# W = w3 @ w_out in float32 matmuls, with its two weights narrowed straight into place

## The chip, the core and the metric

The kernel runs on one core of one Trainium2 chip. The metric is the device time of one execution in microseconds, as a median of repeated runs. The engines are TensorE (PE in the profile, its weight loads PEld), VectorE (DVE), ScalarE (ACT), GpSimd (POOL) and SyncE (SP), which issues the DMAs.

## What is computed

The reference runs three layers, one behind the other, over 3072 tokens of width 384 (4 sequences of 768, 8 heads of 48):

```
# 1. linear attention with decay w and bonus u, per head a 48x48 state
y[t] = r[t] @ (state + (u*k[t]) v[t]);  state = w*state + k[t] v[t]
# 2. mixture of 8 experts: one expert per token, tokens with x @ w_skip <= 0 pass through
out = x + gate * (relu(x @ w1[e]) @ w2[e])
# 3. second MLP, d_ff = 1024
h = (x @ w1) * (x @ w2) @ w3
return (h @ w_out).astype(np.float32)
```

In layer 3 nothing stands between `@ w3` and `@ w_out`, so the kernel computes the 1024x384 product W = w3 @ w_out once and uses `(a*b) @ W`. Its weights w1, w2, w3 and w_out arrive as float64 and are narrowed to float32 on the chip.

## The kernel before

The program has three stages, each in an order of instructions that is written out by hand; every engine takes its own in that order.

**Attention** goes over 24 tiles of 128 tokens (two chunks of 64, of two sequences). The loop at L822 runs n = 0 to 21; the last two tiles and the last routing are done step by step in the list at L875, called the tail here. Iteration n prepares tile n+2 (`prep` L392: DVE writes FB, POOL writes kt; `prep_k` L406: POOL writes ku), computes the scores of tile n+1 on PE (`scores` L450) and masks them on DVE (`evac` L459), then computes y of tile n (`y_mm` L465), transposes tile n-1 and takes its router logits (PE output T), and updates the state (`ds_mm` L480, PE output S). The routing of a group of tiles (`route_a`, `route_b`, `route_c`) adds some twenty small DVE instructions to five of the iterations.

**W** is made in between. A job is a quarter of w_out (L310, "o") or a row block of w3 ("3"); there are 4 and 8. `w_step` (L703), called two or three times in an iteration, takes a job on by one step: ACT makes the magnitude (`magnitude` L117), DVE does three instructions on a work tile `nar` (`narrow` L126: L133, L136, L140), then ACT casts the high part (L167, `wo_hi` or `w3_hi`) and POOL subtracts for the low part (L171, `wo_lo` or `w3_lo`), while DVE is at the next job. All 12 low parts go to POOL, by `w_eng` (L700) and LOP. `w_mm` (L728) gives the matmuls of W one by one: a row block takes 24 of 384 columns, three for each of the 8 contraction blocks (high by high, high by low, low by high), in float32r, which is one pass each. The finished block is split again into W_hi (ACT, L713) and W_lo (DVE, L721).

**Filling.** PE is not kept busy by the attention's small matmuls. `fill_at` (L760) stands behind each pair of them and keeps an account, `debt`, of how many columns are wanted (a rate R[n] for each iteration, in columns per microsecond) and how many were issued. Where the account is positive it puts in a burst: three matmuls of W, or, as long as W's weights are not ready, six matmuls of 256 columns on zeros (`idle_mm`, L753; called dummies here). `keep` (L771) puts in a fixed number of them in the tail.

**Experts** start at L915 with the gather of the first tokens (`load_x`, DMA `xr`), their transposes (`pT`) and a loop over 64 pieces of weights (`mm1` PE output hp, `mm2` PE output y). What is left of W is done between those transposes and the first `mm1` (L948). **The second MLP** (L1162) follows.

Of the kernel before, what the change touches and what calls it, by code (L numbers as in the profile page):

```python
# [18 lines left out]
P = 128  # L19
# [21 lines left out]
R = (1180, 1060, 950, 1000, 1030, 1150, 1150, 1090, 1150, 1000, 1150, 1180, 1300, 1240, 1270, 1350, 1350, 1210, 1400, 1400, 1400, 1270, 1270)  # L41
# [10 lines left out]
KW = 4  # L52
W0 = 3
# [22 lines left out]
def fused_kernel(ctx, tc, att, rk, vn, wt, u, wg, we, w3, wo, w12, r, k, v, wu, out):  # L76
# [14 lines left out]
    # an expert's slots: gate, the token to read, the token to write (none: out of bounds)  # L91
# [14 lines left out]
    def load_wide(pool, tag, src):  # L106
        """Loads [P, n] of a weight and gives it as float32."""
        k = src.shape[1]
        if not wide:
            raw = pool.tile([P, k], F32, tag=tag, name=tag, bufs=2)  # L110
            nc.sync.dma_start(out=raw, in_=src)
            return raw
        raw = pool.tile([P, k, 2], I32, tag=tag, name=tag, bufs=2)
        nc.sync.dma_start(out=raw.rearrange("p n w -> p (n w)"), in_=src.bitcast(I32))
        return raw

    def magnitude(raw, pool):  # L117
        """First step of narrowing float64 words, (low, high) pairs. The high word as a float32 has the upper 8 of the
        float64's 11 exponent bits: 2^-112 less is 1023 - 127 less in all 11."""
        if not wide:  # L120
            return raw
        t = pool.tile([P, raw.shape[1]], I32, tag="nar", name="nar", bufs=2)
        nc.scalar.activation(out=t.bitcast(F32), in_=raw[:, :, 1].bitcast(F32), func=AF.Abs, scale=2.0 ** -112)
        return t

    def narrow(raw, t):  # L126
        """The other steps, and where the result is."""
        if not wide:
            return [], t
# [13 lines left out]
        return [shift, low, sign], t.bitcast(F32)  # L143

    def prep_steps(jobs, pool, eng):
        """Weights made ready as high and low parts, in steps of about one instruction on VectorE, the other engines'
        for the weights before and after between them. A job: what was loaded, a function that gives the places of high
        and low or None if it can't yet, what to do when the load was read, when high is there and when low is."""
        back = []

        def front():
            job = next(jobs, None)
            return job and job + (magnitude(job[0], pool),)
# [26 lines left out]
        while job:  # L180
            raw, places, used, end_hi, end_lo, t = job
            ops, x = narrow(raw, t)
# [35 lines left out]
    def ring_pair():  # L218
        # the last pieces leave ring 0 to the way into the second MLP
# [8 lines left out]
    # ------------------------------------------------------------ attention  # L228
# [3 lines left out]
    wo_hi = wop.tile([P, NF, D], F32R, name="wo_hi")  # L232
    wo_lo = wop.tile([P, NF, D], F32R, name="wo_lo")
# [8 lines left out]
    with tc.manual_schedule():  # L242
# [7 lines left out]
        # natural-layout decay of even chunks, the bonus u, the decay of odd chunks  # L250
# [67 lines left out]
        # decay tables: U[:, h, i] = w^(i-64), Tm[:, h, j] = w^(63-j)  # L318
# [35 lines left out]
        # of each token: its number + 1 in two parts, its gate in three  # L354
        val = ac.tile([P, NT, 5], BF16, name="val")

        def consts():
            """Constants that the first tiles don't need; in steps."""
# [25 lines left out]
        # ---- per chunk pieces  # L384
# [7 lines left out]
        def prep(n):  # L392
            """Decayed r and k: r into both planes of F."""
# [12 lines left out]
        def prep_k(n):  # L406
            c2 = n // 2 % 2
            kn = blobs[n][:, D:2 * D]
            # the last chunks' states are of no use
# [55 lines left out]
        def y_mm(n, tag="y"):  # L465
# [6 lines left out]
            for h in range(NH):  # L472
                # the next head's first columns ride along
# [85 lines left out]
        def route_b(gi):  # L559
            """A token's rank in its expert: the tokens before, in the tile and in the tiles before."""  # L560
# [23 lines left out]
        def route_c(gi):  # L584
            """Of a token's slot: the lane, and whether it is in one of the 16 tiles (beyond CAP: no such lane)."""
# [15 lines left out]
        def route_d(gi, eng):  # L601
            """The gate's parts."""
# [23 lines left out]
        def place(k, t):  # L626
            """What the slots of the next tokens get."""
# [19 lines left out]
        def place_all(gi, eng):  # L647
            """The last ones: first the tokens' numbers."""
# [31 lines left out]
        # ---- W = w3 @ w_out: weights made ready in small steps, matmuls between the attention's  # L680
        w3_ = {}

        def w_jobs():
            """w_out's quarters and w3's row blocks."""
            for i, (kind, q) in enumerate(jobs):
                def places(kind=kind, q=q):
                    if kind == "o":
                        return [a[:, 2 * q:2 * q + 2].rearrange("p g d -> p (g d)") for a in (wo_hi, wo_lo)]
                    if q - 2 >= n_w[0]:
                        return None  # L690
                    w_eng[0] = nc.gpsimd if q < 4 or LOP[q - 4] else nc.vector
                    w3_[q] = [wop.tile([P, NF, P], F32R, tag=x, name=x, bufs=2) for x in ("w3_hi", "w3_lo")]
                    return [a.rearrange("p g f -> p (g f)") for a in w3_[q]]

                yield (raw_w.pop(0), places, lambda i=i: load_w(i + 2), lambda j=(kind + "h", q): fresh[1].append(j),
                       lambda j=(kind, q): fresh[1].append(j))
# [3 lines left out]
        w_eng = [nc.gpsimd]  # L700
        wprep = prep_steps(w_jobs(), nrp, lambda: w_eng[0])
# [7 lines left out]
        def w_evac(k):  # L709
            """Takes a finished row block of W out of PSUM."""  # L710
# [17 lines left out]
        def w_mm():  # L728
            for f in range(NF):
                ps = None  # L730
                i = 0
                for g, low in [(g, False) for g in range(NF)] + [(g, True) for g in range(NF)]:
                    while not (("3", f) in done if low else ("o", g // 2) in done and ("3h", f) in done):
                        yield False
                    if ps is None:
# [5 lines left out]
                        hi, lo = w3_.pop(f)  # L741
                    for a, b in ((lo, wo_hi),) if low else ((hi, wo_hi), (hi, wo_lo)):
                        nc.tensor.matmul(ps, a[:, g], b[:, g], start=(i == 0), stop=(i == 3 * NF - 1))  # L743
                        i += 1
                        yield True
# [4 lines left out]
        debt = [0.0, 0]  # L750
# [9 lines left out]
        def fill_at(us, act):  # L760
            """Part of W, or of nothing while W's weights are not ready, where the matmuls in between (their time, and
            columns with rows and passes as weights) are too thin for the tensor engine's clock to stay up."""
            debt[0] += rate[0] * us - act
            if debt[0] >= 0:
                for _ in range(BURST):
                    debt[1] = bool(next(wmm, None))
                    if not debt[1]:
                        idle_mm()
                debt[0] += BURST * (rate[0] * (0.163 if debt[1] else 0.218) - (384 if debt[1] else 512))

        def keep(k):  # L771
            """Matmuls of W, or of nothing."""
            for _ in range(k):
                if not next(wmm, None):
                    idle_mm()

        # ---- pipeline
# [92 lines left out]
        # the last two, with the banks that are free now  # L870
# [29 lines left out]
        # general path wanted: a decay out of the tables' range, or an expert with over CAP tokens  # L900
# [5 lines left out]
    # ------------------------------------------------------------ experts  # L906
# [510 lines left out]
```

## Time and profile before

| | |
|---|---|
| median of 3 runs | 709.45 us (708.15 to 711.8) |
| span of the profiled execution | 712.7 us |
| PE busy in the span | 648.3 us (91%) |
| DVE busy | 431.4 us (61%) |
| ACT busy | 290.5 us (41%) |
| POOL busy | 234.3 us (33%) |

The profile gives the span of one execution, from its first instruction to its last, and nothing of what lies around it; that span is 3.25 us above the median of the three timed runs. The shares are means over stages that differ. The attention's loop lasts until about 207 us, its tail until 238 us, the experts until 401 us, and the second MLP to the end. A row of the timeline gives the start and the duration of an instruction. A small float32 matmul leaves two records, one behind the other.

### The profile page before, as it was taken

How to read it: one execution, taken by the hardware profiler on the slowest of the kernel's cores; microseconds unless marked ns; L12 is line 12 of the kernel's file. 1: busy time of each engine (PE TensorE's matmuls, PEld its weight loads, DVE VectorE, ACT ScalarE, POOL GpSimd, SP SyncE). 2: the span in 40 equal slices, each digit the busy share in tenths (PEclk: the TensorE clock that was granted, in tenths of full speed). 3: DMA queues.
4: the chain of work that ended last, by engine and by line, in shares of the span. 5: the costliest groups of instructions: out<-in, count | busy, mean ns of one | idle time of the engine just before them, and what ended most of it. 6: DMA issues, size and time to landing. Idle time of an engine off the chain costs nothing.

```text
span 712.7 us, 13497 instructions
## 1 busy us (share of the span) xinstructions
PE 648.3 (91%) x5398; PEld 577.3 (81%) x5398; DVE 431.4 (61%) x705; ACT 290.5 (41%) x634; POOL 234.3 (33%) x175
## 2 busy tenths in 40 slices
PE   8798588697898899989988999999999999999996
PEld 6677476586687799989988789889889889889886
DVE  8779999998998668989987432132232231230330
ACT  4556554544463465656643422232232222221220
POOL 7889658634643355556632200000000000000000
PEclk9888768878999899999999999999999999999999
DMA  8998778677531687776851100200200100101001
GB/s 203 274 244 245 193 208 228 196 203 204 161 112 28 228 287 228 245 264 236 273 194 61 62 1 17 72 1 22 67 1 34 56 1 34 55 1 46 0 1 49
DMA packets 32647, 89.71 MB, mean 126 GB/s; under 512 B 5257, under 2 KB 19226, under 8 KB 31552
## 3 DMA queue, kind: packets, MB, share of 16 engines
q1 hardware_dynamic: 30528, 83.33, 38.6%
q0 software_dynamic: 2048, 5.44, 2.2%
q8 instruction: 44, 0.72, 0.4%
q14 instruction: 27, 0.22, 0.1%
HBM read 77.02 MB, written 12.58 MB: 126 GB/s over the span
## 4 chain that ended last, share of the span: by engine, by line
PE 54%; DVE 22%; DMA 10%; issue 9%; POOL 2%; ACT 2%; SPq 0%; DVEq 0%; POOLq 0%; ACTq 0%
PE ab L1182 28%; PE po L1200 14%; DMA TB<-in_att 5%; PE hp L983 3%; DVE nar L136 3%; DVE elo L102 2%; PE wp L743 2%; PE y L1002 2%; DMA raw<-in_we 2%; DVE nar L140 2%; DVE nar L133 2%; DVE hl L987 1%; DVE FB L463 1%; DVE FB L403 1%; DVE FB L462 1%
## 5 line engine op out<-in xcount | busy, mean ns | idle before, releaser
L1182 PE MATMUL ab<-bxh,w12h 128*128 128x512 f32 x288 | 112.4, 390 | 0.6 <-ACT bxh L1220 0.6
L1182 PE MATMUL ab<-bxh,w12l 128*128 128x512 f32 x288 | 112.1, 389 | 0.0
L1182 PE MATMUL ab<-bxl,w12h 128*128 128x512 f32 x288 | 112.0, 390 | 0.0
L1189 DVE TENSOR_TENSOR p_sb<-ab,a_sb 128x512 f32<-128x512 f32 x48 | 33.2, 692 | 123.5 <-PE ab L1182 123.5
L1190 ACT CAST ph<-p_sb 128x512 fp32r<-128x512 f32 x48 | 29.8, 620 | 105.7 <-DVE p_sb L1189 105.7
L1200 PE MATMUL po<-W_hi,ph 128*128 128x384 f32 x192 | 66.7, 348 | 0.0
L1200 PE MATMUL po<-W_hi,pl 128*128 128x384 f32 x192 | 65.0, 339 | 0.0
L1200 PE MATMUL po<-W_lo,ph 128*128 128x384 f32 x192 | 65.0, 338 | 0.0
L983 PE MATMUL hp<-xh,ehi 128*128 128x256 f32 x192 | 56.5, 296 | 8.9 <-DVE hl L987 8.8
L1182 PEld LDWEIGHTS ab<-bxh,w12h 128*128 128x128 f32 x288 | 54.1, 188 | 12.6 <-ACT bxh L1220 1.6
L1182 PEld LDWEIGHTS ab<-bxl,w12h 128*128 128x128 f32 x288 | 54.1, 188 | 11.7 <-DVE bxl L1222 0.4
L1182 PEld LDWEIGHTS ab<-bxh,w12l 128*128 128x128 f32 x288 | 54.1, 188 | 10.8
L411 POOL TENSOR_TENSOR ku<-blob,KU 128x768 f32<-128x768 f32 (+1 forms) x24 | 47.6, 1985 | 36.5 <-PE S L489 27.7
L983 PE MATMUL hp<-xl,ehi 128*128 128x256 f32 x192 | 54.7, 287 | 0.0
L983 PE MATMUL hp<-xh,elo 128*128 128x256 f32 x192 | 54.6, 287 | 0.0
L101 ACT CAST ehi<-raw 128x768 fp32r<-128x768 f32 x64 | 52.6, 828 | 4.5 <-DMA raw<-in_we 4.5
L1191 DVE TENSOR_TENSOR pl<-p_sb,ph 128x512 fp32r<-128x512 f32 x48 | 33.2, 693 | 32.9 <-ACT ph L1190 32.9
L102 POOL TENSOR_TENSOR elo<-raw,ehi 128x768 fp32r<-128x768 f32 x22 | 42.4, 1927 | 20.1 <-ACT ehi L101 19.8
L986 ACT ACTIVATE hh<-hp 128x256 fp32r<-128x256 f32 x64 | 24.6, 385 | 56.9 <-PE hp L983 56.7
L439 ACT ACTIVATE zv<-VS,z 128x48 f32<-128x48 f32 x184 | 43.9, 321 | 8.4 <-DVE z L426 6.3
L475 PE MATMUL y<-VS,FB 112*64 112x64 f32 (+3 forms) x384 | 32.0, 240 | 16.3 <-ACT VS L447 10.7
L983 PEld LDWEIGHTS hp<-xh,ehi 128*128 128x128 f32 x192 | 37.6, 197 | 11.4 <-DVE hl L987 11.3
(221 smaller groups left out, 1667.4 us busy)
## 6 DMA issues: line engine op xcount, KB each, us to landing
raw<-in_we SPq DMA_DIRECT2D x32, 768.0 KB, 5.0
TB<-in_att SPq DMA_DIRECT2D x48, 192.0 KB, 5.6
blob<-in_rk SPq DMA_DIRECT2D x24, 384.0 KB, 6.5
raww<-in_w SPq DMA_DIRECT2D x8, 1024.0 KB, 6.6
raw<-in_w SPq DMA_DIRECT2D x8, 768.0 KB, 6.7
VS<-in_vn SPq DMA_DIRECT2D x24, 192.0 KB, 3.6
xm<-xg SPq DMA_DIRECT2D x48, 96.0 KB, 3.3
out<-ob SPq DMA_DIRECT2D x24, 192.0 KB, 1.9
```

Of the source, the lines that this page charges most:

```text
L101: nc.scalar.copy(out=hi, in_=raw)
L102: (eng or nc.vector).tensor_tensor(out=lo, in0=raw, in1=hi.bitcast(F32), op=ALU.subtract)
L411: nc.gpsimd.tensor_tensor(out=ku_[n][:, a:b], in0=kn[:, None, :].to_broadcast([P, b - a, D]), in1=KU[:, c2 + a:c2 + b], op=ALU.mult)
L439: nc.scalar.activation(out=zv[:, h], in_=vs[:, 0, h], func=AF.Copy, scale=z[:, h:h + 1])
L475: nc.tensor.matmul(yv[0:64, h, 0:w], F[a, 0, h], vf[a, 0, HD * h:HD * h + w], start=True, stop=True)
L983: nc.tensor.matmul(hp, a, b, start=(i == 0), stop=(i == 8))
L986: nc.scalar.activation(out=hh, in_=hp, func=AF.Relu)
L1182: nc.tensor.matmul(q, a, b, start=(i == 0), stop=(i == 8))
L1189: nc.vector.tensor_tensor(out=p_sb, in0=ps[1], in1=a_sb, op=ALU.mult)
L1190: nc.scalar.copy(out=ph, in_=p_sb)
L1191: nc.vector.tensor_tensor(out=pl, in0=p_sb, in1=ph.bitcast(F32), op=ALU.subtract)
L1200: nc.tensor.matmul(po, a[:, P * t:P * t + P], b[:, f], start=(i == 0), stop=(i == 3 * NF - 1))
```

## The change

w_out and w3 are no longer split. The magnitude of a job and its three DVE instructions are written straight into `wo_s` (w_out, 8 blocks of 384) or into a w3 tile of which there are three, and the 12 casts on ACT and the 12 subtractions on POOL are gone. The matmuls of W take float32 operands: 8 for a row block instead of 24, each four passes where a float32r matmul is one. W itself is split into W_hi and W_lo as before, and the later stages are as they were.

The filling changes with it. A burst is now one matmul of W (counted as 4 times 384 columns), or six dummies as before; the rates R are 1200 for iteration 7 and 1480 for 8 to 21, where 1000 to 1400 stood. `keep` counts a matmul of W as four units.

```diff
-R = (1180, 1060, 950, 1000, 1030, 1150, 1150, 1090, 1150, 1000, 1150, 1180, 1300, 1240, 1270, 1350, 1350, 1210, 1400, 1400, 1400, 1270, 1270)
+R = (1180, 1060, 950, 1000, 1030, 1150, 1150, 1200) + (1480,) * 14
+W3B = 3
...
-    wo_hi = wop.tile([P, NF, D], F32R, name="wo_hi")
-    wo_lo = wop.tile([P, NF, D], F32R, name="wo_lo")
+    wo_s = wop.tile([P, NF, D], F32, name="wo_s")
...
+        def w_steps():
+            def front(i):
+                if i == len(jobs):
+                    return None
+                kind, q = jobs[i]
+                if kind == "o":
+                    x = wo_s[:, 2 * q:2 * q + 2].rearrange("p g d -> p (g d)")
+                elif q - W3B >= n_w[0]:
+                    return None
+                else:
+                    w3_[q] = wop.tile([P, NF, P], F32, tag="w3", name="w3", bufs=W3B)
+                    x = w3_[q].rearrange("p g f -> p (g f)")
+                raw = raw_w.pop(0)
+                if wide:
+                    magnitude(raw, x.bitcast(I32))
+                    return narrow(raw, x.bitcast(I32))
+                return [lambda: nc.scalar.copy(out=x, in_=raw)]
+
+            ops = None
+            for i, job in enumerate(jobs):
+                while ops is None:
+                    ops = front(i)
+                    if ops is None:
+                        yield
+                now, ops = ops, None
+                for k, op in enumerate(now):
+                    op()
+                    if k + 1 == len(now):
+                        load_w(i + 2)
+                        fresh[1].append(job)
+                    if ops is None:
+                        ops = front(i + 1)
+                    yield
...
-                    for a, b in ((lo, wo_hi),) if low else ((hi, wo_hi), (hi, wo_lo)):
-                        nc.tensor.matmul(ps, a[:, g], b[:, g], start=(i == 0), stop=(i == 3 * NF - 1))
-                        i += 1
-                        yield True
+                        w3 = w3_.pop(f)
+                    nc.tensor.matmul(ps, w3[:, g], wo_s[:, g], start=(g == 0), stop=(g == NF - 1))
+                    yield True
...
             if debt[0] >= 0:
-                for _ in range(BURST):
-                    debt[1] = bool(next(wmm, None))
-                    if not debt[1]:
+                debt[1] = bool(next(wmm, None))
+                if debt[1]:
+                    debt[0] += rate[0] * 0.64 - 4 * D
+                else:
+                    for _ in range(BURST):
                         idle_mm()
-                debt[0] += BURST * (rate[0] * (0.163 if debt[1] else 0.218) - (384 if debt[1] else 512))
+                    debt[0] += BURST * (rate[0] * 0.218 - 512)
...
-            for _ in range(k):
-                if not next(wmm, None):
+            due[0] += k
+            while due[0] > 0:
+                if next(wmm, None):
+                    due[0] -= 4
+                else:
                     idle_mm()
+                    due[0] -= 1
```

Three places in the order of instructions follow, before and after at each; in the changed kernel the lines of the attention stand one lower, and those behind the diff's new functions some twenty higher.

GpSimd, in the attention's loop: kt and ku are the decayed keys of a tile, and w_lo is the low part of a row block of w3. Before:

```order
L419 TENSOR_TENSOR ku<-ku,blob 128x384
L171 TENSOR_TENSOR w_lo<-nar,w_hi 128x1024
L401 TENSOR_TENSOR kt<-TB_110,Tm 128x512
L411 TENSOR_TENSOR ku<-blob,KU 128x768
L419 TENSOR_TENSOR ku<-ku,blob 128x384
L171 TENSOR_TENSOR w_lo<-nar,w_hi 128x1024
```

After:

```order
L418 TENSOR_TENSOR ku<-ku,blob 128x384
L400 TENSOR_TENSOR kt<-TB_109,Tm 128x512
L410 TENSOR_TENSOR ku<-blob,KU 128x768
L418 TENSOR_TENSOR ku<-ku,blob 128x384
L400 TENSOR_TENSOR kt<-TB_110,Tm 128x512
```

The subtractions are gone, and the keys of successive tiles follow each other.

TensorE, iteration 16, from the last y to the transposes (T takes the router logits of L522 and the transposes of L508; wp is the PSUM bank of a row block of W). Before:

```order
L476 MATMUL y<-VS_0_102,FB_107 64x48
L522 MATMUL T<-wgs,xT 128x9 x2
L743 MATMUL wp_113<-wo_hi,w_hi 128x384
L743 MATMUL wp_113<-wo_lo,w_hi 128x384
L743 MATMUL wp_113<-wo_hi,w_hi 128x384
L522 MATMUL T<-wgs,xT 128x9
L508 MATMUL T<-ident,xg 128x128 x3
```

After:

```order
L475 MATMUL y<-VS_0_101,FB_106 64x48
L521 MATMUL T<-wgs,xT 128x9
L761 MATMUL wp_113<-wo_s,w_1675 128x384
L521 MATMUL T<-wgs,xT 128x9 x2
L761 MATMUL wp_113<-wo_s,w_1675 128x384
L507 MATMUL T<-ident,xg 128x128 x3
```

One burst of three float32r matmuls has become two of one float32 matmul.

TensorE, the end of the tail and the start of the experts (S here takes the last slots' sums, pT the transposes of the gathered tokens, G dummies, hp the first expert matmul). Before, with one more dummy and then hp behind it:

```order
L644 MATMUL S_206<-kt 128x48
L743 MATMUL wp_114<-wo_hi,w_lo 128x384 x4
L933 MATMUL pT<-ident,xr 128x128 x6
L743 MATMUL wp_114<-wo_hi,w_lo 128x384 x4
L279 LDWEIGHTS zb
L279 MATMUL G<-zb 128x256
```

After, behind seven more dummies:

```order
L278 LDWEIGHTS zb
L278 MATMUL G<-zb 128x256
L956 MATMUL pT<-ident,xr 128x128 x6
L1006 MATMUL hp<-xh,ehi 128x256 x3
L1006 MATMUL hp<-xh,elo 128x256 x3
L1006 MATMUL hp<-xl,ehi 128x256 x3
```

W is complete before the transposes, and nothing stands between them and the first expert matmul.

## Rows read from the trace of the kernel before

**Rows 1.** Windows, stages: length, busy PE, PEld, DVE, ACT, POOL; clock, DMA share, GB/s

```profile
45.20:207.50 162.30, 131.62 (x1976) 109.72 (x1976) 156.48 (x240) 86.34 (x239) 105.64 (x64) 0.82 0.71 203
207.50:238.40 30.90, 24.95 (x236) 21.97 (x235) 24.06 (x93) 10.27 (x22) 10.40 (x10) 0.93 0.30 97
238.40:401.10 162.70, 150.97 (x1029) 146.77 (x1027) 137.02 (x187) 90.49 (x166) 81.49 (x53) 0.96 0.62 208
```

**Rows 2.** Windows: iteration 9; sums of ten short iterations, seven long, and 9 to 13

```profile
76.60:90.80 14.20, 7.12 (x112) 6.38 (x114) 13.90 (x24) 7.25 (x24) 6.86 (x5) 0.63 0.62 171
...
sum 75.30, PE 69.13 PEld 57.90 DVE 71.36 ACT 44.84 POOL 54.04; mean PE 6.91 PEld 5.79 DVE 7.14 ACT 4.48 POOL 5.40
...
sum 87.00, PE 62.49 PEld 51.82 DVE 85.12 ACT 41.51 POOL 51.60; mean PE 8.93 PEld 7.40 DVE 12.16 ACT 5.93 POOL 7.37
...
sum 49.90, PE 37.34 PEld 31.54 DVE 48.40 ACT 25.64 POOL 31.41; mean PE 7.47 PEld 6.31 DVE 9.68 ACT 5.13 POOL 6.28
```

**Rows 3.** Line 171: ns min/median/max, first and last start in us, forms

```profile
L171 POOL TENSOR_TENSOR w_lo<-nar,w_hi x8: 2348/2366/2802, 66.9 to 219.5; 128x1024 fp32r<-128x1024 f32 x8
L171 POOL TENSOR_TENSOR wo_lo<-nar,wo_hi x4: 1808/1813/2277, 54.0 to 106.0; 128x768 fp32r<-128x768 f32 x4
```

**Rows 4.** Timeline of DVE: instructions beside a subtraction of line 171

```profile
54.33 2.03 DVE L133 TENSOR_SCALAR nar<-nar 128x1024 int32<-128x1024 int32 x1
...
133.82 2.80 DVE L133 TENSOR_SCALAR nar<-nar 128x1024 int32<-128x1024 int32 x1
...
156.50 3.33 DVE L136 SCALAR_TENSOR_TENSOR nar<-raww,nar 128x1024 int32<-128x1024 int32 x1
...
219.61 2.38 DVE L623 TENSOR_TENSOR s_v<-r_o,val 128x80 bf16<-128x80 bf16 x1 [0.49 <-POOL val L610]
```

**Rows 5.** Timeline of DVE: the same with POOL idle; line 463 over all

```profile
203.08 0.68 DVE L133 TENSOR_SCALAR nar<-nar 128x1024 int32<-128x1024 int32 x1
...
126.02 1.23 DVE L136 SCALAR_TENSOR_TENSOR nar<-raww,nar 128x1024 int32<-128x1024 int32 x1
...
222.07 0.23 DVE L623 TENSOR_TENSOR s_v<-r_o,val 128x80 bf16<-128x80 bf16 x1
...
L463 DVE TENSOR_TENSOR FB<-sc,mask x19: 694/694/698, 44.4 to 210.8; 64x512 f32<-64x512 f32 x19
```

**Rows 6.** Timeline of PE: bursts between scores and between logits, dummies

```profile
152.75 0.22 PE L455 MATMUL sc<-FB,kt 64*64 64x64 f32 x1
...
153.18 0.34 PE L743 MATMUL wp<-wo_hi,w_hi 128*128 128x384 f32 x1
...
153.35 0.33 PE L743 MATMUL wp<-wo_lo,w_hi 128*128 128x384 f32 x1
...
153.62 0.27 PE L454 MATMUL sc<-FB,kt 64*64 64x64 f32 x1
...
219.74 0.42 PE L743 MATMUL wp<-wo_hi,w_hi 128*128 128x384 f32 x1
...
220.34 0.51 PE L522 MATMUL S<-wgs,xT 128*128 128x9 f32 x4
...
64.13 0.22 PE L454 MATMUL sc<-FB,kt 64*64 64x64 f32 x1
...
64.19 0.22 PE L454 MATMUL sc<-FB,kt 64*64 64x64 f32 x1
64.34 0.83 PE L279 MATMUL wp<-zb 128*128 128x256 bf16 x6
65.09 0.27 PE L454 MATMUL sc<-FB,kt 64*64 64x64 f32 x1
```

**Rows 7.** Timeline of PE, then of ACT: from the transposes to the experts

```profile
236.34 1.63 PE L743 MATMUL wp<-wo_hi,w_lo 128*128 128x384 f32 x4
...
238.07 0.78 PE L983 MATMUL hp<-xh,ehi 128*128 128x256 f32 x2
...
236.72 0.48 ACT L934 CAST xh<-pT 128x384 fp32r<-128x384 f32 x1 [1.44 <-PE pT L933]
```

More of the change, by code (lines that the diff above doesn't have):

```diff
@@ L115, in load_wide, with magnitude @@
         return raw
[L117 to L122, printed above, removed]
+    def magnitude(raw, t):
         nc.scalar.activation(out=t.bitcast(F32), in_=raw[:, :, 1].bitcast(F32), func=AF.Abs, scale=2.0 ** -112)
@@ L126, in narrow @@
     def narrow(raw, t):
-        if not wide:
-            return [], t
         wl, wh = raw[:, :, 0], raw[:, :, 1]
@@ L141, in sign @@
                                            op0=ALU.bitwise_and, op1=ALU.bitwise_or)
-        return [shift, low, sign], t.bitcast(F32)
+        return [shift, low, sign]
     def prep_steps(jobs, pool, eng):
@@ L152, in front @@
             job = next(jobs, None)
-            return job and job + (magnitude(job[0], pool),)
+            if not job or not wide:
+                return job and job + (job[0],)
+            t = pool.tile([P, job[0].shape[1]], I32, tag="nar", name="nar", bufs=2)
+            magnitude(job[0], t)
+            return job + (t,)
         def go_back():
@@ L181, in prep_steps @@
             raw, places, used, end_hi, end_lo, t = job
-            ops, x = narrow(raw, t)
+            ops, x = (narrow(raw, t), t.bitcast(F32)) if wide else ([], raw)
             after = []
@@ L681, in fused_kernel @@
         w3_ = {}
[L683 to L696, printed above, removed]
         done, fresh = set(), [[], []]
         n_w = [0]
-        w_eng = [nc.gpsimd]
-        wprep = prep_steps(w_jobs(), nrp, lambda: w_eng[0])
+        def w_steps():
[30 more added lines that the diff above has]
+                    yield
+        wprep = w_steps()
         def w_step(k):
@@ L730, in w_mm @@
                 ps = None
-                i = 0
-                for g, low in [(g, False) for g in range(NF)] + [(g, True) for g in range(NF)]:
-                    while not (("3", f) in done if low else ("o", g // 2) in done and ("3h", f) in done):
+                for g in range(NF):
+                    while not (("o", g // 2) in done and ("3", f) in done):
                         yield False
@@ L740, in w_mm @@
                         ps = wp[wf[0]][:, 0:D]
-                        hi, lo = w3_.pop(f)
-                    for a, b in ((lo, wo_hi),) if low else ((hi, wo_hi), (hi, wo_lo)):
-                        nc.tensor.matmul(ps, a[:, g], b[:, g], start=(i == 0), stop=(i == 3 * NF - 1))
-                        i += 1
-                        yield True
+                        w3 = w3_.pop(f)
+                    nc.tensor.matmul(ps, w3[:, g], wo_s[:, g], start=(g == 0), stop=(g == NF - 1))
+                    yield True
                 n_w[0] += 1
@@ L749, in fused_kernel @@
         wmm = w_mm()
-        debt = [0.0, 0]
+        debt, due = [0.0, 0], [0]
         rate = [R0]
```

## The prediction

> **What bounds the kernel now.** I read the windows by stage first, since the shares of the whole span are means over stages with different limits. In the attention's loop [rows 1] DVE is busy 156.5 of 162.3 us and PE 131.6, at a mean granted clock of 0.82; POOL is busy 105.6, ACT 86.3. The reader is to see two engines near their limit, and one of them at a clock that falls to the lower level (1.2 GHz instead of 2.4) for part of the time. In the experts [rows 1] PE is busy 151.0 of 162.7 us, and the change leaves that stage as it is, so I take it that what the attention and its tail gain or lose moves the end by as much.
>
> Next I cut the loop into iterations (by the first scores matmul of each) and sorted those from 5 to 21, in which W is made, into two kinds [rows 2]. In ten short ones (7, 8, 11 to 14, 16, 18, 19, 21; 6 to 9 us each) PE is busy 69.1 of 75.3 us, DVE 71.4: both bind. In seven long ones (5, 6, 9, 10, 15, 17, 20) DVE is busy 85.1 of 87.0 us and PE 62.5: DVE binds, and PE has 24.5 us of room. Iteration 9 stands for them: DVE 13.9 of 14.2 us, PE 7.1, clock 0.63.
>
> Last I looked at why DVE is so long. An instruction of DVE takes its time by what POOL does beside it. The shift of line 133 takes 0.68 us with POOL idle [rows 5] and 2.80 us beside a subtraction of line 171 [rows 4]; the routing's product of 128x80 takes 0.23 and 2.38 us. Line 463, which reads PSUM, takes 694 to 698 ns always [rows 5]. The change takes those subtractions away, 12 of them: 8 of about 2.4 us and 4 of about 1.9 [rows 3], 27.1 us of POOL.
>
> **Part 1: the subtractions go; DVE.** Eight DVE instructions are stretched by line 171 (from what they take there what they take alone) [rows 4, 5]: 54.33, 2.03 - 0.68 = 1.35 us; 133.82, 2.80 - 0.68 = 2.12; 156.50, 3.33 - 1.23 = 2.10; 219.61, 2.38 - 0.23 = 2.15; and four more of the same pattern with 1.34, 1.43, 2.16 and 1.43. That is 14.1 us: 8.3 in the long iterations, 3.6 in the short ones, 2.15 in the tail. Where DVE binds this is time off the path, but not all of it: behind each subtraction POOL has kt and ku queued, which move up and meet other DVE instructions. From none to all of 8.3 is possible in the long iterations; I take three quarters, **-6.3 us**, since POOL's whole work falls by a quarter (27.1 of 105.6 us) and kt and ku meet DVE in any case.
>
> The Trainium skill ("SBUF — State Buffer", section "Who interferes with whom") says that DVE and GpSimd share one pair of ports, that whoever issues first holds it for the whole instruction and that the other fully blocks; an operand in PSUM does not need it. Rows 4 and 5 agree (2.80 against 0.68 us; 0.69 us always). By that rule the relief of a DVE instruction is lost again wherever kt or ku gets the pair next, which is my third rival below.
>
> **Part 2: ACT and the order of preparation.** ACT loses 12 casts; it is busy 86.3 of 162.3 us [rows 1], and I cost that at nothing. If PE waits for a state copy behind such a cast, this is a gain of a few tenths, which I leave out. A job now costs the same three DVE instructions and is finished one to two steps earlier, and its load (one DMA of SP's queue, 768 or 1024 KB) is issued one iteration earlier. The DMA share in the loop is 0.71 [rows 1], so I cost that at nothing too; if the early load delays a tile's own loads, it costs up to the time of one load, some microseconds, once.
>
> **Part 3: the matmuls of W; PE.** A float32r matmul of 384 columns comes 0.17 us behind the one before (153.18, 153.35) [rows 6]. No float32 matmul of that size is in the trace. The nearest are the scores, 64 columns: two records each, 0.06 us apart (64.13, 64.19). Scaled to 384 columns that gives 2 x 6 x 0.057 = 0.68 us; the lower end is two float32r passes, 0.35 us. I take 0.68, by the row that is float32 itself. The 8 row blocks then take 64 x 0.68 = 43.5 us against 192 x 0.175 = 33.6.
>
> The Trainium skill ("FP8 and Floating Point Precision", section "TensorE Precision Notes") says that true float32 takes four passes through the array. By it a product costs 4 x 384 columns where it cost 3 x 384, an estimate of 0.64 us at 2.4 GHz, and it speaks against this change. With 0.64 in place of 0.68 the sum below would be some 0.4 us lower.
>
> What PE pays is the burst with its switches. Three float32r matmuls between scores take from 152.75 to 153.62, 0.87 us, of which 0.35 is switching; between logits, from 219.74 to 220.34, 0.60 us, of which 0.08 is [rows 6]. One float32 matmul: 0.68 + 0.35 = 1.03 and 0.68 + 0.08 = 0.76, 0.9 in the mean (the bursts sit about evenly in both). Six dummies take from 64.19 to 65.09, also 0.9 [rows 6]. So a burst costs about what it did, and what counts is their number. From the order of instructions I count 44 bursts in iterations 6 to 21 before and 64 after (84 dummies after where there were 24): in the ten short iterations 11 more, in the long ones 9 more (4 in iteration 9, 3 in 10, 2 in 17).
>
> In the long ones 9 x 0.9 = 8.1 us lie within PE's 24.5 us of room: nothing. In the short ones 11 x 0.9 = 9.9 us meet 75.3 - 69.1 = 6.2 us of room [rows 2]: **+3.7 us**. Its ends are +9.9 (no room is usable) and -3.6 (the clock rises, all fits, and DVE's relief counts).
>
> **Part 4: the tail.** DVE's instruction at 219.61 loses 2.15 us, and what follows it (the last logits' copies and the last routing) is in DVE's order behind it. PE has one more burst in the last scores and eleven float32 matmuls in the tail's routing in place of 32 float32r ones, by the prices above some 1.5 us more in front of those logits; **-0.65 us** is left (0 to -2.15). Later bursts are dummies beside DVE's own work: nothing. Behind the transposes four matmuls of W (at the lower clock) and two dummies hold the first expert matmul until 238.07, though its input is there at 236.72 + 0.48 = 237.20 [rows 7]: **-0.8 us**, as W is complete by then.
>
> **The sum.** -6.3 + 3.7 - 0.65 - 0.8 = -4.05 us. The profiled execution's span, 712.7 us, becomes 708.65; the trace shows nothing around it, and it stands 3.25 us above the median of the runs, 709.45. I put the same difference on the median: 709.45 - 4.05 = **705.4 us**, own range 701 to 709. What is late next in the long iterations is still DVE, in the short ones PE.
>
> **Rivals.** First, **PE's clock recovers and DVE alone sets the loop.** The denser filling raises the granted clock above 0.82; PE's work is 131.6 x 0.82 + 20 x 0.9 = 126 us at the full one, and 162.3 - 11.9 = 150.4 us are left, so it fits. Then all relief counts: -8.3 - 3.6 - 2.15 - 0.8 = -14.9, 694.6 us. For it: DVE at 96% of the loop. Against it: in the short iterations PE has little room even at a clock of 1, and in the long ones the clock falls because PE waits for DVE, which filling in front of the wait does not cure.
>
> Second, **slower: the bursts run at the lower clock.** Iterations 9 to 13 get 13 more bursts, most of them dummies (iteration 10 alone has 30). If the clock there stays as low as iteration 9's 0.63, a burst costs about 1.8 us (six dummies take twice as long at 1.2 GHz): 23.4 us against a room of 49.9 - 37.3 = 12.6 [rows 2], +10.8. The rest: relief in the other long iterations, three quarters of 5.6, -4.2; five more bursts in the other short ones past their room, +1.4; the tail -1.45. Sum +6.55, 716.0 us. It decides from the point where the clock in that stretch is below about 0.8. For it: the clock in iteration 9. Against it: more columns in the stretch are what the filling is there for, and rows 2 show PE idle in a quarter of it.
>
> Third, **the relief is handed back**: kt and ku move into the place of the subtractions and stretch DVE as these did. Part 1 gives 0, the others stay: +3.7 - 1.45 = +2.25, 711.7 us. For it: POOL still has some 80 us of such work beside a DVE that is never idle. Against it: the stretch is only made by what runs, and a quarter less runs.
>
> That the change does not do what it says is no rival: the order shows the subtractions gone.
>
> **How the numbers follow.** Forecast 0.43, first rival 0.18, second 0.22, third 0.17. A measurement of this kernel can tell about 0.5%, 3.5 us, from no change: faster is below 705.9, slower above 713.0. Faster: 0.18 and somewhat more than half of the forecast's 0.43, 0.44. Slower: most of the second rival's 0.22 and the upper end of the third, 0.22. The same: 0.34. The range reaches to the first rival's and the second's own times, 694.5 to 716: beyond them lie no more than half of each, 0.2 together.
>
> **What would show it.** Right: line 133 at 0.7 to 1.7 us instead of up to 2.8; the long iterations shorter by about 6 us together; the short ones longer by about 4, with PE busy throughout; the first hp right behind the cast xh; the experts and the second MLP as long as before. The first rival: a clock above 0.9 in 45 to 207 us and DVE with hardly any wait for PE. The second: 76 to 126 us longer than before, at a clock of 0.8 or less, DVE waiting for the scores. The third: DVE's busy time unchanged, with kt and ku beside the long instructions. I am wrong in the price of W if its records are not about 0.34 us apart, two to a matmul.

## The result

The changed kernel takes 714.4 us (median of 13 runs), the kernel before 710.8 in the same sessions: a ratio of 1.0055, 95% interval 1.0032 to 1.0078. The prediction was 705.4 us with a range of 694.5 to 716.0. The time lies in the range, but on the other side: 4.05 us of gain were forecast, and 3.9 of loss were measured (0.55% of 710.8; the two profiled spans, 712.7 and 716.6 us, differ by as much). Here and below a median in us takes in all runs of a kernel, and a ratio leaves out the few that were slower than the rest.

The windows by stage of the changed kernel, cut where [rows 1] are: iterations 5 to 21, the tail, the experts. Columns: length, busy PE, PEld, DVE, ACT, POOL; granted clock, DMA share, GB/s.

```profile
50.90:213.90 163.00, 144.31 (x2020) 104.69 (x2016) 128.53 (x242) 78.54 (x228) 75.35 (x51) 0.88 0.68 197
213.90:243.90 30.00, 25.00 (x241) 18.16 (x239) 18.80 (x89) 7.00 (x17) 6.20 (x8) 1.00 0.25 76
243.90:404.80 160.90, 150.91 (x1028) 145.54 (x1028) 135.68 (x187) 90.24 (x165) 81.46 (x53) 0.97 0.63 214
```

Against [rows 1] DVE has lost 28 us of work in the loop (156.5 to 128.5), POOL 30, and the clock rose from 0.82 to 0.88; yet the stretch is as long as before (163.0 against 162.3), and it begins 5.7 us later (50.9 against 45.2). DVE is now busy in 79% of it and PE in 89%, so neither fills it: waits have come in. Those of iterations 4 to 21 name the one that matters. First after, then before; columns: who waits for whom, us in total, times, longest.

```profile
PEld y L474 <- ACT VS L446: 20.0, 5, 6.9
ACT xT L513 <- PE T L507: 17.1, 8, 4.0
ACT w L121 <- DMA raww<-in_w: 16.4, 4, 5.9
...
ACT wo_s L121 <- DMA raww<-in_wo: 10.2, 3, 5.7
```

```profile
PEld y L475 <- ACT VS L447: 10.2, 4, 7.2
...
ACT nar L123 <- DMA raww<-in_wo: 1.4, 1, 1.4
ACT nar L123 <- DMA raww<-in_w: 1.2, 2, 1.0
```

Line 121 (123 before) is the magnitude, the first step of narrowing a weight. ACT waits 26.6 us in it for the weight's load, where it waited 2.6. Seven jobs of twelve are hit. One of them, in iteration 7, of the changed kernel: the timeline of SP's queue, of ACT, of PEld and of DVE (start, length, instruction, idle time before it and what ended it).

```profile
61.01 0.54 SPq L115 DMA_DIRECT2D raww<-in_wo  x1
```

```profile
62.18 0.62 ACT L414 COPY FB<-FB 64x512 f32<-64x512 f32 x1 [2.61 <-DVE FB L402]
68.49 0.89 ACT L121 ACTIVATE wo_s<-raww 128x768 f32<-128x768 f32 x1 [5.69 <-DMA raww<-in_wo]
69.28 1.90 ACT L438 ACTIVATE zv<-VS,z 128x48 f32<-128x48 f32 x8
71.08 0.45 ACT L513 COPY xT<-T 128x384 f32<-128x384 f32 x1
71.56 0.47 ACT L446 COPY VS<-S 48x384 f32<-48x384 f32 x1
```

```profile
72.09 0.29 PEld L474 LDWEIGHTS y<-VS,FB 112*64 112x64 f32 x2 [6.03 <-ACT VS L446]
```

```profile
66.48 1.16 DVE L132 SCALAR_TENSOR_TENSOR wo_s<-raww,wo_s 128x768 int32<-128x768 int32 x1
71.57 0.17 DVE L525 COPY L<-T 128x9 f32<-128x9 f32 x1 [3.92 <-ACT xT L513]
```

The reader is to see a queue. The load is issued at 61.01; ACT reaches the magnitude at 62.80 and stands there until the load has landed at 68.49. Behind it in ACT's order are eight zv, xT and the state copy VS, none of which waits again. PE cannot begin y without VS (6.03 us idle), DVE cannot go on without xT (3.92). PE's idle time then costs the clock too: it is granted in full (1.00) from 57.4 to 69.5, and from 69.5 to 80.0 at the lower of its two levels.

```profile
69.50:80.00 10.50, 7.89 (x93) 6.54 (x95) 6.20 (x12) 6.88 (x24) 1.49 (x2) 0.51 0.58 180
```

Iteration 7 takes 15.4 us (6.0 before); 4, 10 and 13 are hit in the same way (13.7, 14.7 and 14.0 us against 7.3, 11.9 and 8.7). Of those in between, 5, 6 and 9 are shorter than before (6.5, 6.6 and 7.5 us against 9.2, 9.0 and 14.2), 12 is about as long, and 8 and 11 are a little longer (7.3 and 7.4 against 7.2 and 6.4).

Why the magnitude stands there: the old generator called it behind the third of a job's three steps, because the first two were taken up by the high and low part of the job before. With no parts left, the new generator calls it behind the first step, two steps (one iteration) earlier. The load did not move along by as much: two buffers hold the raw weights, so it is issued behind the last step of the job two before, in the new generator at the end of that step and in the old one at the start of the next. Where three steps lay between the load and the magnitude, little more than one is left. In the kernel before, 5.2 to 17.8 us passed from the issue of a load to the moment when ACT came to its magnitude; in the seven jobs that are hit it is 1.3 to 3.8 us.

### The profile page after: what moved, and what is told of

It reads as the page before. It is cut to its first block, busy times and chain, and to the rows that moved or that the text cites. A ratio compares the mean times of both kernels' runs of the same rounds, so it can differ in the third digit from the quotient of the medians.

```text
span 716.6 us, 13554 instructions
## 1 busy us (share of the span) xinstructions
PE 661.5 (92%) x5444; PEld 567.8 (79%) x5444; DVE 402.3 (56%) x705; ACT 280.1 (39%) x622; POOL 203.0 (28%) x163
## 4 chain that ended last, share of the span: by engine, by line
PE 62%; DVE 16%; DMA 9%; issue 8%; ACT 3%; SPq 1%; POOL 0%; DVEq 0%; ACTq 0%; POOLq 0%
PE ab L1205 27%; PE po L1223 14%; PE hp L1006 6%; PE y L1025 4%; PE wp L761 3%; DMA raww<-in_w 3%; DMA VS<-in_vn 2%; DVE elo L103 1%; ACT zv L438 1%; DMA TB<-in_att 1%; DMA xm<-xg 1%; DVE hl L1010 1%; DVE FB L462 1%; PE T L521 1%; PE pT L1185 1%
## 5 line engine op out<-in xcount | busy, mean ns | idle before, releaser
L410 POOL TENSOR_TENSOR ku<-blob,KU 128x768 f32<-128x768 f32 (+1 forms) x24 | 44.9, 1870 | 76.8 <-PE S L488 66.3
L1205 PEld LDWEIGHTS ab<-bxh,w12h 128*128 128x128 f32 x288 | 54.0, 188 | 12.6 <-ACT bxh L1243 1.6
L761 PE MATMUL wp<-wo_s,w 128*128 128x384 f32 x128 | 62.9, 578 | 0.0
L1009 ACT ACTIVATE hh<-hp 128x256 fp32r<-128x256 f32 x64 | 24.7, 386 | 57.4 <-PE hp L1006 57.1
```

Of the source, the lines that this page charges most:

```text
L410: nc.gpsimd.tensor_tensor(out=ku_[n][:, a:b], in0=kn[:, None, :].to_broadcast([P, b - a, D]), in1=KU[:, c2 + a:c2 + b], op=ALU.mult)
L761: nc.tensor.matmul(ps, w3[:, g], wo_s[:, g], start=(g == 0), stop=(g == NF - 1))
L1205: nc.tensor.matmul(q, a, b, start=(i == 0), stop=(i == 8))
```

## Experiments

The figures are ratios to the kernel before, measured beside it, each with its 95% interval, and then the median. Theory Q is the queue just shown; theory P says that the 20 more bursts and the float32 matmuls are the loss; theory L that the earlier load takes bandwidth from the tiles' own.

**The magnitude put back** (e1_late_magnitude), in the changed kernel:

```
-                    if ops is None:
+                    if k + 1 == len(now):
                         ops = front(i + 1)
```

> The changed kernel, with one line moved: the magnitude of the next job is issued behind a job's last step instead of behind its first, so that it stands two steps later in ACT's order, as in the kernel before. Loads, matmuls and rates stay. Theory Q (the magnitude stands in ACT's in-order queue before its load has landed, and the state copies and zv behind it wait): ACT's waits for raww in the loop fall from 26.6 us to under 4, PE's waits for VS with them, and the loop becomes 6 to 10 us shorter: 704 to 708 us, ratio to before 0.990 to 0.996. Theory P (the 20 more bursts and the float32 matmuls are the loss): about as the changed kernel, 714, ratio 1.005. Theory L (the earlier load takes bandwidth from the tiles' own loads): as the changed kernel too, 714, since the loads are issued where they were.

Measured: 0.987 (0.982 to 0.992), 700.6 us: 1.85% or 13.2 us less than the changed kernel, more than Q had said. The waits of its loop; those for raww in w are gone from the list:

```profile
ACT wo_s L121 <- DMA raww<-in_wo: 2.5, 2, 2.0
...
PEld y L474 <- ACT VS L446: 1.4, 1, 1.4
```

The clock of the loop rises to 0.92 and it becomes 14.4 us shorter (163.0 to 148.6):

```profile
45.40:194.00 148.60, 137.14 (x2020) 100.03 (x2016) 134.65 (x242) 78.52 (x228) 78.12 (x53) 0.92 0.78 220
```

Loads, bursts and rates are the same, so neither P nor L can explain this difference.

**The early magnitude alone** (e2_before_early), in the kernel before (a flag to the old generator, and a third buffer for nar):

```
-                elif not after:
+                if (early or not b) and not after:
                     after.append(front())
```

> The kernel before, with the magnitude of the next job behind a job's first step, where the changed kernel has it, and a third buffer for its result. Everything else, the subtractions and three passes too, stays. Theory Q: ACT waits some 20 us for raww in the loop where it waited 2.6, and the time rises by 4 to 9 us, to 715 to 720, ratio 1.006 to 1.013. Theories P and L: no change, 711, ratio 1.000, since neither the matmuls nor the loads move.

Measured: 1.024 (1.020 to 1.028), 728.3 us, some 17 us more where Q had named 4 to 9. ACT's waits for raww in its loop:

```profile
ACT nar L123 <- DMA raww<-in_w: 37.4, 6, 9.7
...
PEld y L476 <- ACT VS L448: 20.3, 5, 8.5
...
ACT nar L123 <- DMA raww<-in_wo: 17.0, 3, 7.8
```

So the move costs time without anything else of the change. Its 17 us are not its price in the changed kernel: the old generator issues a load one step later than the new one, so here the magnitude stands nearer to it still. ACT comes to it from 2.3 us before the issue to 6.5 us after it in the jobs that wait for a load, and waits 54.4 us in all, where the changed kernel's ACT waits 26.6.

**An earlier load in place of a later magnitude** (e3_third_buffer), in the changed kernel:

```
-LW = (0, 1)
+LW = (0, 1, 2)
...
-            raw = pool.tile(..., bufs=2)
+            raw = pool.tile(..., bufs=3 if tag == "raww" else 2)
...
-                        load_w(i + 2)
+                        load_w(i + 3)
```

> The changed kernel with three buffers for the raw weights in place of two, each load issued one job earlier; the magnitude stays where the change put it. Theory Q: the load lands before ACT comes to the magnitude, ACT's waits for raww fall under 4 us, 704 to 708 us, ratio 0.990 to 0.996. Theory P: no change against the changed kernel, 714, 1.005. Theory L: the loads are earlier still, 714 or more.

Measured: 0.987 (0.983 to 0.991), 702.4 us, with 3.8 us of waits for raww in the profile. The same loss is cured from the other end, and loads that are a job earlier still cost nothing that can be seen: L falls.

**Part 1 alone** (e4_no_low_parts), in the kernel before (low parts of w_out and w3 left out):

```
-                eng().tensor_tensor(out=out[1], in0=x, in1=out[0].bitcast(F32), op=ALU.subtract)
+                if pool is not nrp:
+                    eng().tensor_tensor(out=out[1], in0=x, in1=out[0].bitcast(F32), op=ALU.subtract)
...
-                    for a, b in ((lo, wo_hi),) if low else ((hi, wo_hi), (hi, wo_lo)):
+                    for a, b in ((hi, wo_hi),) if low else ((hi, wo_hi), (hi, wo_hi)):
```

> The kernel before without the subtractions of line 171 for W's weights: the low parts of w_out and w3 are left out, the matmuls that read them read the high parts in their place, as many as before. This is part 1 of the prediction alone. By the prediction (three quarters of the relief in the long iterations, most of the tail's): -6.3 to -8, so 703 to 705 us, ratio 0.989 to 0.992. If all relief counts: -14, 697, ratio 0.980. If kt and ku hand it back: 711, ratio 1.000.

Measured: 0.977 (0.974 to 0.981), 695.2 us: 16.2 us of gain, more than if all of the counted relief had counted. The windows of its loop and tail, and from DVE's timeline the longest instruction of line 133 within the loop, now 1.75 us:

```profile
47.50:192.50 145.00, 125.04 (x1982) 103.44 (x1978) 138.37 (x242) 85.96 (x238) 84.04 (x54) 0.87 0.79 227
192.50:221.10 28.60, 24.13 (x235) 21.34 (x234) 19.75 (x91) 9.62 (x20) 5.81 (x8) 0.93 0.32 105
```

```profile
155.28 1.75 DVE L133 TENSOR_SCALAR nar<-nar 128x1024 int32<-128x1024 int32 x1
```

DVE's busy time in the loop falls by 18.1 us and the loop by 17.3. I summed over both traces what DVE instructions take beyond the shorter ones of their form, by the POOL instruction beside them (loop and tail). Before: about 17 us beside line 171 and 40 beside kt, ku and FB; here about 35 beside kt, ku and FB. So nothing was handed back, and kt and ku stretch a little less too. This run takes away one thing more, which it does not separate: in the kernel before, POOL's own queue stood still for ACT's casts, with kt and ku behind the subtraction that waited (iterations 4 to 21):

```profile
POOL w_lo L171 <- ACT w_hi L167: 15.8, 4, 5.3
```

That DVE's busy time falls by as much as the loop speaks for the stretch as the larger share; how much the queue adds is not shown.

**The filling.** The rates of the kernel before, in e1_late_magnitude (e5_old_rates):

```
-R = (1180, 1060, 950, 1000, 1030, 1150, 1150, 1200) + (1480,) * 14
+R = (1180, 1060, 950, 1000, 1030, 1150, 1150, 1090, 1150, 1000, 1150, 1180, 1300, 1240, ...)
```

> e1_late_magnitude with the rates R of the kernel before. In iterations 6 to 21 there are then 37 matmuls of W and no dummies, where e1_late_magnitude has 50 and 84 (14 bursts); 13 matmuls of W are left behind the last transposes. If PE binds the short iterations with every burst at 0.9 us and little room: the loop 8 to 12 us shorter than in e1_late_magnitude, the tail 5 to 9 us longer, together 697 to 703 us, ratio to before 0.981 to 0.990, and the loop's gain is what the denser filling costs. If the filling lies in PE's room or is paid back by the clock: the loop as long as there, the tail longer, 706 to 709, ratio 0.993 to 0.998.

Measured: 0.985 (0.980 to 0.991), 701.8 us, no better than with the changed rates. The stages of its profile:

```profile
46.90:184.30 137.40, 118.92 (x1902) 91.06 (x1898) 125.48 (x231) 74.10 (x222) 78.22 (x53) 0.86 0.83 235
184.30:225.50 41.20, 32.70 (x226) 21.01 (x224) 26.26 (x98) 10.66 (x22) 5.85 (x8) 0.96 0.22 73
```

The loop is 11.2 us shorter than in e1_late_magnitude, the tail 10.7 longer: what is filled in is work of the tail, done early, at about its own price.

The other way round, the changed rates in e4_no_low_parts, with three float32r matmuls a burst (e6_new_rates_only; the edit of R as above, from the old rates to the changed ones):

> e4_no_low_parts (low parts of w_out and w3 left out) with the rates R of the changed kernel: three float32r matmuls a burst as before, but as many bursts as the changed rates ask for. Against e4_no_low_parts (ratio 0.977) this is part 3 of the prediction without float32. By the prediction some 20 more bursts cost 3.7 us: ratio 0.981 to 0.984, 697 to 700 us. If none of PE's room is usable, 18 us: 1.000. If the filling pays for itself by the clock: 0.977 or less.

Measured: 0.987 (0.981 to 0.994), 701.6 us. The expectation had the count wrong: with three small matmuls to a burst these rates ask for 79 bursts in iterations 6 to 21, 35 more than before and not 20. They cost 1.0% or 7 us, 0.2 us for each; the two intervals leave some 5 us either way.

Then fewer dummies, in e1_late_magnitude (e7_fewer_dummies) and, with the magnitude left early, in the changed kernel (e11_early_few_dummies):

```
-R = (1180, 1060, 950, 1000, 1030, 1150, 1150, 1200) + (1480,) * 14
+R = (1180, 1060, 950, 1000, 1030, 1150, 1150, 1150) + (1200,) * 5 + (1480,) * 9
```

> e1_late_magnitude with the rates of iterations 7 to 12 lowered to 1150 and 1200: 2 bursts of dummies where there were 14, the matmuls of W later on as there (48 before the tail in place of 50). If PE binds these iterations: 12 bursts of 0.9 us less, half of it in PE's room, 5 to 6 us shorter than e1_late_magnitude, 695 to 697, ratio 0.978 to 0.981. If the dummies keep the clock up: the granted clock in iterations 7 to 12 falls, and the time stays at 701 or above, ratio 0.987 or more.

> The changed kernel, magnitude where the change put it, with the rates of e7_fewer_dummies. Theory Q: ACT's waits for raww stay at 20 us or more and the fewer bursts lie in the time that PE waits for the state copies: 0.999 to 1.006, so that e7_fewer_dummies against this one shows the early magnitude at 2.4 to 3%. Theory P (the bursts were the loss): the 1.2% that they give in e7_fewer_dummies against e1_late_magnitude is had here too, ratio 0.993.

Measured: 0.975 (0.970 to 0.981) with the late magnitude, 695.7 us, faster than both kernels by more than any interval here; and 0.993 (0.990 to 0.997) with the early one. So the rates are worth 1.2% in either place and the magnitude 1.8 to 1.85% with either rates. The expectation that the waits would swallow the bursts was wrong: P's part of the loss is real, beside Q's. The 12 bursts are worth 8.5 us here, 0.7 us for each. In the profile of the former the clock in iterations 7 to 12 does fall, as the rival had it, and the stretch is shorter all the same. First e1_late_magnitude, then e7_fewer_dummies:

```profile
57.60:108.90 51.30, 48.16 (x755) 37.22 (x749) 48.20 (x79) 28.05 (x83) 30.44 (x21) 0.93 0.89 253
```

```profile
60.90:109.50 48.60, 42.39 (x667) 32.63 (x667) 46.89 (x84) 28.56 (x84) 28.51 (x19) 0.81 0.89 262
```

**Mixtures.** Both cures (e8_both_cures); both cures and the fewer dummies (e9_cures_and_rates); the magnitude behind the second step (`if ops is None and k > 0`) with the changed rates (e10_one_step) and with the fewer dummies (e12_one_step_few):

> The changed kernel with both cures: three buffers for the raw weights (loads a job earlier) and the magnitude behind the last step. Theory Q: each cure alone leaves 2.5 to 3.8 us of ACT's waits for raww; together about none, 699 to 701 us, ratio 0.984 to 0.987. If the two cures did something else each (buffers, order) their gains would add: 0.970 to 0.975.

> e8_both_cures with the rates of e7_fewer_dummies: magnitude behind the last step, three raw buffers, 2 bursts of dummies in iterations 6 to 12. Theory Q with PE binding those iterations: as e7_fewer_dummies or up to 3 us better, 692 to 696 us, ratio 0.971 to 0.976. If the third buffer gives nothing once the order is right: equal to e7_fewer_dummies, 0.975.

> The changed kernel with the magnitude behind a job's second step: one step later than the change has it (ratio 1.0055), one earlier than e1_late_magnitude (0.987). Theory Q: a step is 3 to 5 us, so ACT's waits for raww are about half of 26.6 us, 8 to 15, and the ratio lies between, 0.992 to 1.001. If only the order against one certain instruction counts, it is one of the two ends.

> e10_one_step (magnitude behind the second step) with the rates of e7_fewer_dummies. If order and filling add as parts of their own: the 1.2% that fewer bursts give with the magnitude at either end come on top of 0.980, ratio 0.968, 690 us. If behind the second step some waits for raww stay and the fewer bursts only expose them: 0.975 to 0.980, no better than e7_fewer_dummies.

Measured: 0.977 (0.970 to 0.984); 0.984 (0.980 to 0.988); 0.980 (0.974 to 0.987); 0.981 (0.975 to 0.986). Both cures together lie between what was expected of one thing cured twice (0.984 to 0.987) and of two gains that add (0.970 to 0.975), and the interval reaches both, so that this run alone does not decide; two things speak for one loss: in the profile of e8_both_cures no wait for raww is left, where e1_late_magnitude had 2.5 us, so that the second cure finds next to nothing to cure; and with the fewer dummies both cures are no better than the late magnitude alone (0.984 against 0.975). One step later is as good as two, although 12.6 us of waits stay there (the waits of e10_one_step):

```profile
ACT w L121 <- DMA raww<-in_w: 9.0, 5, 4.5
...
ACT wo_s L121 <- DMA raww<-in_wo: 3.6, 2, 2.9
```

I had expected half the loss for half the waits; that up to some point they are covered by other work would explain it, and is not shown. The fewer dummies give 1.2% in e7_fewer_dummies and e11_early_few_dummies and nothing in e9_cures_and_rates and e12_one_step_few. Why is open: e7 to e10 and e12 lie within 1% of each other, and their intervals touch or nearly touch.

## Why the prediction was wrong

Along three kernels the change is taken in steps (as parts of 711 us): before to e4_no_low_parts, the subtractions, **-16.2 us**; from there to e1_late_magnitude, everything else of the change (20 more bursts, float32, narrowing in place, the casts gone, the tail), **+7.0**; from there to the changed kernel, the early magnitude, **+13.2**. The sum is +4.0, as measured; the intervals leave some 3 us either way on the first step and 4 on each of the others. The prediction had -8.45, +4.4 and 0 for them (part 1 with the 2.15 of DVE in the tail; 3.7 + 1.5 - 0.8; part 2). That 714.4 us still lies in its range is luck: a gain nearly twice as large as forecast made up for more than half of a loss that it did not know.

**Part 1** foretold the mechanism and not its size: -6.3 us in the loop and -2.15 of DVE in the tail, against -16.2. Three quarters of the long iterations' relief was too little, and the relief was more than 14.1 us (about 17 beside line 171, and some 5 less beside kt, ku and FB). The reason for the caution, that kt and ku would take the place, is refuted. The sign, line 133 at no more than 1.7 us, is met in the loop of e4_no_low_parts (1.75) and not quite in the changed kernel, where the longest (line 129 there) takes 2.1 us. Relief in the short iterations, which the sum left to PE, seems to have counted as well: the loop became 17.3 us shorter, and DVE had been busy in 96% of it.

**Part 2** is the step that failed. It took the earlier finish of a job as free and looked for its price in bandwidth only: "if the early load delays a tile's own loads, it costs up to the time of one load". In e3_third_buffer, where the loads are a job earlier still, that price cannot be seen (0.987, as with e1_late_magnitude). What had moved was the magnitude, an ACT instruction that waits for a DMA, and it had moved farther than its load (the loads of iterations 5 to 9 are issued 0 to 6 us earlier than before). Nothing in the prediction says what is queued behind it on ACT. ACT's share, 86.3 of 162.3 us, was read as room; but an engine that is half idle still blocks all that stands behind an instruction that waits. e1_late_magnitude gives the term as 13.2 us, with ACT's waits for raww 26.6 us with it and 2.5 without; the prediction's own sum would have been +9 with it.

**Part 3** had the price of a burst right, but did not use it throughout, and its room holds for the kernel before alone. The timeline of PE in the changed kernel: a burst between logits and the transposes of xg, one between scores, and two products one behind the other in the tail:

```profile
152.14 0.89 PE L761 MATMUL wp<-wo_s,w 128*128 128x384 f32 x2
152.87 0.49 PE L507 MATMUL T<-ident,xg 128*128 128x128 f32 x3
```

```profile
155.44 0.22 PE L453 MATMUL sc<-FB,kt 64*64 64x64 f32 x1
155.59 0.91 PE L761 MATMUL wp<-wo_s,w 128*128 128x384 f32 x2
156.44 0.27 PE L453 MATMUL sc<-FB,kt 64*64 64x64 f32 x1
```

```profile
226.93 1.54 PE L761 MATMUL wp<-wo_s,w 128*128 128x384 f32 x4
228.30 0.51 PE L521 MATMUL S<-wgs,xT 128*128 128x9 f32 x4
```

Counted as in the prediction, a burst takes 0.73 us between logits, where 0.76 was forecast, and 1.00 between scores (155.44 to 156.44), where it was 1.03. There are two records to a matmul, as foretold, but up to 0.43 us apart where the burst stands between other matmuls (155.59 and 156.02), and not 0.34: by the prediction's own sign its price of the product was off, and the price of the burst came out all the same. Three float32r matmuls took 0.60 and 0.87 [rows 6], so a burst of W became 0.13 us dearer in both places. The prediction said that a burst costs about what it did and counted only the 20 new ones; on the 40 bursts of W that iterations 6 to 21 have before, that leaves out some 5 us of PE (an estimate, 40 x 0.13). By the Trainium skill's four passes ("FP8 and Floating Point Precision", section "TensorE Precision Notes") I had estimated 0.64 us for the product alone. The trace agrees: the two in the tail take 1.37 us from the first start to the start of what follows, 0.64 each with 0.08 for the switch, and not the 0.68 that the sum used.

What the 20 more bursts and float32 cost together is in the +7.0 us between e4_no_low_parts and e1_late_magnitude, where 4.4 were forecast; the difference is within the intervals. A new burst was forecast at 3.7 us / 20, near the 0.2 us of e6_new_rates_only; in the state of e1_late_magnitude and of the changed kernel the last 12 cost 0.7 us each (e7_fewer_dummies, e11_early_few_dummies). Once DVE is relieved, PE has no room left in most of the former long iterations (137.1 of 148.6 us busy in the loop of e1_late_magnitude, and all the time in 5, 9, 10, 15 and 17). Part 1 and Part 3 were each worked out against the other's state of before.

**Part 4** came about as foretold: the tail 30.0 us against 30.9, DVE 18.8 against 24.1 (e4_no_low_parts has 28.6 us, so that PE's part costs 1.4 us, where 1.5 was forecast), and the first hp directly behind the last cast (where [rows 7] have 0.87 us between them):

```profile
243.38 0.48 ACT L957 CAST xh<-pT 128x384 fp32r<-128x384 f32 x1 [1.61 <-PE pT L956]
```

```profile
243.91 1.01 PE L1006 MATMUL hp<-xh,ehi 128*128 128x256 f32 x3 [0.57 <-ACT xh L957]
```

**The rivals.** The first (DVE's whole relief counts, clock above 0.9) foretold 694.6 us; e1_late_magnitude has the clock, 0.92 in the loop, and with 700.6 us lies between this rival and the forecast. In the changed kernel the queue hid it. The second foretold 716.0, the nearest figure, by a mechanism that did not happen: iterations 9 to 13 take 52.0 us against 49.9, but at a clock of 0.87 and not of 0.8 or less, and two of them (10 and 13) are among those that the queue makes longer:

```profile
86.80:138.80 52.00, 45.60 (x630) 34.16 (x624) 40.27 (x75) 24.08 (x68) 22.74 (x15) 0.87 0.69 203
```

The third is refuted: DVE's busy time in the loop fell by 28 us. The case that came true stood among none of them.

## What to carry over

When a generator loses some of its steps, list where each of the remaining instructions now stands on its engine, and for each that waits for a DMA set the distance from the load's issue to that place against the time a load takes to land (here 4.4 to 9.4 us, mostly 5 to 8); then read what is queued behind it. A half-idle engine is no cover for an instruction that waits: ACT's queue stopped whole for 5.7 us in iteration 7. And where a change relieves the binding engine, price its other parts on the profile as it will be then, not on the one of before.

## What the runs showed beside that

A wait of 5.7 us in one engine's queue came with an iteration 9.4 us longer (iteration 7, 15.4 us; 6.0 before and in e1_late_magnitude): PE's idle time is followed by 10.5 us at the lower clock (0.51), so that the work behind it is slower as well.

The experts' stage, which no kernel here changes, took 152.9 us (e6_new_rates_only), 153.8 (e5_old_rates), 159.5 (e1_late_magnitude), 160.9 (after), 162.7 (before) and 163.7 (e4_no_low_parts). In e5_old_rates this gives back half of what the longer tail costs. That what the attention gains moves the end by as much was good only to some us, and I have not found what sets it.
